# Thirteen runs of 128x128 products sent through four column tiles of TensorE

## The chip, the cores and the metric

The kernel runs on one core of a Trainium2 chip. The metric is the time of one execution on the device, in microseconds (us); lower is better. Three timed runs of the kernel before gave 318.03, 318.08 and 318.10 us; their median, 318.08 us, is the time before.

## The reference

Four batches of 12544 tokens of width 128 pass through two attentions against 32 inducing points, and then through a layer with 1024 hidden units that keeps the larger of two products:

```python
def _attn_ref(x, inducing):                  # x: 4 x 12544 x 128, inducing: 32 x 128
    ...
    def mab(q, kv):
        s = scale * (q @ kv.transpose(0, 2, 1))
        s = s - s.max(-1, keepdims=True)
        a = np.exp(s)
        a /= a.sum(-1, keepdims=True) + 1e-09
        return a @ kv
    h = mab(I, x)                            # 32 points look at all tokens
    return mab(x, h)                         # every token looks at the 32 results

def _moe_ref(x, w1, w2, w_out):              # 50176 x 128; d_ff = 1024
    h1 = x @ w1
    h2 = x @ w2
    g = np.maximum(h1, h2)
    return g @ w_out
```

## The kernel before

**Algebra.** The second attention's output is a mixture of the 32 rows of `h`, so `x @ w1` and `x @ w2` behind it are products with 32 rows too. The kernel writes max(h1, h2) as h1 + relu(h2 - h1). The h1 part is linear and is folded into one small matrix `m1`; the relu part needs `hwd`, which is `h` times (w2 - w1), and then `woutp`, the output weights.

**Tiling.** Tokens are handled in chunks of 128. A `Block` holds four quarters of up to four chunks each. Three kinds of work on TensorE concern us, and each uses the 128x128 array in a mode of its own:

- *Column work*: four matmuls, each of 32 weight columns, side by side, writing to four different groups of 32 PSUM partitions. Such are `stage` (L657: scores of a block's tokens), `pool_scores` (L356: scores of the next batch's 32 points) and `pool_accum` (L414 and L433: the sums of the first attention; its matmuls have 128 rows, 32 weight columns and 128 moving columns).
- *Rounds*: `phase` (L1085), up to four matmuls at a time with 32 rows each, side by side in four row tiles, from `hwd` and the block's exponentials `e`. Each fills one PSUM bank with 128x512 numbers. The relu of each bank is written to SBUF in 16 bits by ScalarE (L1102) or VectorE (L1105), whichever the kernel's own clock model expects to be done earlier. A round may also carry the linear part (`m`, `e`: four 32x128 matmuls).
- *Products*: `final_one` (L932), one matmul of a 128x128 block of `relu` as weights with a 128x128 block of `woutp` moving. There are 3136. Eight for each of a group's chunks accumulate in one PSUM bank (`g.ps`), which `evict_group` scales by the softmax's denominators and stores (L964, L971, L989).

**Order.** The instructions of PE, DVE, ACT, POOL and SP stand in the order in which the program writes them. That order is a string written out by hand, `ORDER`: `s` is one `stage`, `c`, `t`, `a`, `r`, `e`, `h`, `w`, `m` are steps of the first attention of the next batch, `x` a transposing DMA of the next batch, `g` the softmax's denominators by a transposing DMA and POOL, `p4.13` one `phase` of four matmuls with a bit mask that says which of them swap their relu engine, and a bare number is that many products:

```python
elif word.isdigit():
    for _ in range(int(word)):
        ready = final_ready()
        keep_busy(ready)
        ck.wait(ready, "relu")
        final_one()
```

`ck` is the clock model. It decides at build time which bank and which relu engine are taken. It counts a switch of mode (`SWITCH`) and 0.0558 us for a product (`PAIR`). There are eight PSUM banks; a matmul that starts a new bank waits by a semaphore for the engine that read the bank last.

Of the kernel before, what the change touches and what calls it, by code (L numbers as in the profile page):

```python
# [131 lines left out]
def kernel(  # L132
# [9 lines left out]
    nc = tc.nc  # L142
# [3 lines left out]
    NJB = J // 128  # L146
# [25 lines left out]
    def bank(shape, dtype=F32, only=None):  # L172
        i = min(range(8), key=lambda j: ck.bank[j]) if only is None else only
        uid[0] += 1
        return i, psum.tile(shape, dtype, name=f"ps{uid[0]}", tag=f"bank{i}", bufs=1)
# [55 lines left out]
    woutp = consts.tile([128, NJB, C], F16, name="woutp")  # L231
# [6 lines left out]
    with tc.manual_schedule(engines={ET.PE, ET.DVE, ET.Activation, ET.Pool, ET.SP}):  # L238
# [402 lines left out]
        state = {}  # L641
# [107 lines left out]
        def dens(blk):  # L749

            blks = [blk]
            if 0 < blk.index < len(blocks) - 1:
                nxt = blocks[blk.index + 1]
                if nxt.staged is not None and nxt.staged <= ck.pe and nxt.rp is None:
                    blks.append(nxt)
            bi, ps = bank([128, 512])
            ck.wait(ck.bank[bi], "den bank")
            uid[0] += 1
            rp = rpp.tile([128, 8, 4], F32, name=f"rp_{uid[0]}", tag="rp")
            n = 0  # L760
            for blk in blks:
                wd = blk.width
                for t in range(wd):
                    nc.tensor.matmul(
                        out=ps[:, 4 * (n + t) : 4 * (n + t) + 4],
                        lhsT=blk.e2[:, 128 * t : 128 * (t + 1)],
                        rhs=ones_q,
                        start=True,
                        stop=True,
                    )  # L770
                blk.rp = rp[:, n : n + wd, :]
                n += wd
            end = ck.run(0.029 * n)
            nc.vector.reciprocal(out=rp[:, 0:n, :].rearrange("p t q -> p (t q)"), in_=ps[:, 0 : 4 * n])
            ck.bank[bi] = ck.on_dve(end, 0.18 + 0.001 * 4 * n)
# [89 lines left out]
        def final_ready():  # L865
            if state["g"] >= len(groups):
                return INF
            g = groups[state["g"]]
            if g.ps is None and (g.blk.staged is None or len(held) >= HELD):
                return INF  # L870
            t0, u = g.parts[state["mm"] // 4]
            r = g.blk.done.get((g.q, t0, u))
            if r is None:
                return INF
            if g.ps is None:
                r = max(r, min(ck.bank))
            return r
# [25 lines left out]
        def linear_full():  # L903

            g = held[0]
            if st[g.blk.b].get("m1r", INF) > ck.pe or "m1" not in st[g.blk.b]:
                return False
            for s, (q, t) in enumerate(g.chunks):
                nc.tensor.matmul(
                    out=g.ps[:, 128 * s : 128 * (s + 1)],  # L910
                    lhsT=g.blk.e2[:, 128 * t : 128 * (t + 1)],
                    rhs=m1bd[:, q, :],
                    start=False,
                    stop=True,
                    skip_group_check=True,
                )
            evict_group(held.pop(0), ck.run(0.056 * len(g.chunks)))
            return True

        def final_one():  # L920
            g = groups[state["g"]]
            n = len(g.chunks)
            if g.blk.rp is None:
                dens(g.blk)
            if g.ps is None:
                g.bank, g.ps = bank([128, 512])
                ck.wait(ck.bank[g.bank], "group bank")
                ck.bank[g.bank] = INF
            jb, t = g.order[state["mm"]]
            c = g.chunks.index((g.q, t))  # L930
            w4 = g.blk.quarters[g.q].w
            nc.tensor.matmul(  # L932
                out=g.ps[:, 128 * c : 128 * (c + 1)],
                lhsT=g.blk.relu[g.q][:, 128 * (jb * w4 + t) : 128 * (jb * w4 + t + 1)],
                rhs=woutp[:, jb, :],
                start=not g.started,
                stop=(state["mm"] + 1 == n * NJB and g.linear),
                skip_group_check=True,
            )
            g.started = True  # L940
            end = ck.run(ck.PAIR)
            state["mm"] += 1
            state["done"] += 1
            if state["mm"] == n * NJB:
                if g.linear:
                    evict_group(g, end)
                else:
                    held.append(g)
                    if g.full:
                        linear_full()  # L950
                state["g"] += 1
                state["mm"] = 0
# [159 lines left out]
        state["stage"] = 1  # L1112
        ORDER = """
        s p4.13 s H1 W g2 p4.1 p2 8 m0 4 p3 p2.1 10 p3 p2 13 p3.2 6 p4.5 22 p2 p4.8 17 x1.0 p4.8 4 g1 11
        p4.1 13 p4.9 p1 16 p3.4 p2 14 p4.10 6 x1.1 4 x1.2 x1.3 x1.4 x1.5 x1.6 2 p3.6 s s s s 6 g3 6 p4.5
        14 x1.7 1 x1.8 p4.8 19 p4.10 p2.1 12 x1.9 5 p3 14 p4.4 c1.0 15 p1 p4.5 14 p4.3 g4 13 p4.8 25 p4.6
        p3.2 10 x1.10 17 p2 p3.1 15 c1.1 p4.2 12 t1.1 2 p3 6 p4.2 4 g5 11 c1.2 c1.3 p4.1 18 p4.4 t1.3 21
        p3.5 p3 22 c1.4 p1.1 p4.1 19 p2 p4.8 5 g6 21 p4.2 p2 c1.5 19 r1 a1.1 p3.2 p4 t1.5 19 a1.3 p4.9
        p2.2 29 p3.3 p4 26 p4.1 a1.5 5 p3.1 p2.3 1 e1 11 p4.12 1 h1 17 w1 s s s s p3.2 19 m1 15 p4.6 p3.6
        30 p3.1 p3.3 24 p3 p3.3 27 p3.2 p3.1 20 p4.3 p2 15 s p4.1 18 p2.1 p3 15 g7 g8 7 p3.3 p4.2 9 g9 12  # L1120
        x2.0 3 x2.1 x2.2 s p1.1 p4.4 x2.3 12 p4.5 14 p4.6 14 p4 14 p3 21 p3.6 p4.8 14 g10 4 x2.4 4 x2.5
        x2.6 9 p4.13 s c2.0 14 p4.6 p1 5 x2.7 4 x2.8 13 p3.3 p3.4 23 p4.4 11 c2.1 p4 p1 9 t2.1 4 g11 x2.9
        4 x2.10 10 p4.3 p3 15 c2.2 p3.3 21 p3.1 p3.5 27 p3.3 p3.2 c2.3 19 p4.10 4 g12 4 t2.3 5 p4.1 17
        p3.1 p3.4 16 a2.1 c2.4 p3.1 p3.1 23 p4.4 18 p2.1 p4.9 13 g13 17 p4.9 p3.3 24 a2.3 c2.5 p4.1 p2 7
        t2.5 12 r2 18 p3 p4.2 30 p4.10 p2.2 16 a2.5 p4.3 p3.6 8 e2 10 p4.2 2 h2 21 p3.1 p3.6 11 w2 4 m2
        15 p4.11 s s s 13 p3 p2 12 s p4 15 p2 p3.2 22 p3.5 p3.2 3 x3.0 4 x3.1 19 p3.4 p4.12 25 p3.3 13 p3
        p3.3 27 p3.2 p3.5 12 g15 8 g14 3 p4 11 s s p3.1 p2.2 14 x3.2 4 x3.3 4 x3.4 x3.5 5 p3.1 p4.5 19
        x3.6 17 p3.4 p4.1 23 g16 14 p4.4 p3 27 c3.0 s p3.1 15 x3.7 c3.1 p4.2 p1 x3.8 15 p4.4 21 p3.4 p3 8
        g17 14 p3.3 p2 6 t3.1 12 p4.2 p1 20 p3.4 p3.4 22 p4.10 p2.1 30 p4.3 p3 4 g18 8 x3.9 4 x3.10 7
        c3.2 a3.1 c3.3 p4.3 p2 9 t3.3 15 p4.4 17 p2.1 p4.8 27 p2.2 p4.1 13 g19 18 p3.3 p4.4 10 r3 8 c3.4  # L1130
        c3.5 a3.3 p4.5 20 t3.5 1 p4.8 p2.2 21 p4.4 13 p3.5 p2 1 g20 27 p4.4 p3.3 27 a3.5 p4.8 p2.3 2 e3
        16 h3 14 p3.5 p4.2 10 w3 4 m3 15 s p4.1 9 g21 10 p3.1 p2.1 15 p3.5 s s s 13 p3.1 p3.4 22 p4.8 p1
        27 p4.3 p3 9 g22 13 p2.2 p2 22 p3.2 p4.3 25 s s p3.4 13 p3 p3.3 30 p4.9 p3.2 g23 21 p4.2 20 p4.1
        p2.2 30 p3.4 p4.2 24 s p2 p3.2 12 p4.8 g24 22 p4.6 p2.2 20 p2.1 p3.2 16 p3.1 p2 11 p4.9 21 p4.3 9
        p1 p3 g25 p1 20 p3.1 p3.4 30 p4.8 p3.1 26 p4.8 13 p4.6 13 p4.3 9 g26 13 p3.3 p3 27 p3.5 p2 22 p2
        p4.1 22 p2.2 p4.9 22 p3 p2.1 g27 27 p4.1 p3.2 38 p4.3 p3.1 31 p2 p4.9 22 p2.1 p3.1 24 p3 p4.11 40
        p3.4 p3 21 p4.6 21 p2.1 p3.4 31 p4.4 p4.3 63
        """

        EVICT = "000000000000000000000000101000000000000000000000010000000000000000000010000000000000000000000000000000010000"  # L1140
# [17 lines left out]
        for word in ORDER.split():  # L1158
            if word == "s":
                stage(blocks[state["stage"]])  # L1160
                state["stage"] += 1
            elif word.isdigit():
                for _ in range(int(word)):
                    ready = final_ready()
                    keep_busy(ready)
                    ck.wait(ready, "relu")
                    final_one()
            else:
                WORK[word[0]](*[int(n) for n in word[1:].split(".") if n])
        assert state["g"] == len(groups) and not held and state["stage"] == len(blocks)  # L1170
# [31 lines left out]
```

## Time and profile before

| | value |
|---|---|
| median of three timed runs | 318.08 us (318.03 to 318.10) |
| the profiled execution's own time | 317.76 us |
| its span | 316.0 us |
| TensorE matmul (PE) busy | 308.6 us, 5308 records |
| VectorE (DVE) busy | 274.5 us |
| ScalarE (ACT) busy | 280.2 us |
| GpSimd (POOL) busy | 125.8 us |

The span is the time from the first to the last instruction that the profiler recorded in that execution. PE busy is the union of the recorded spans of all matmuls. Matmuls overlap, and their recorded ends are modelled, so the distance between their starts tells more than their lengths. PEld is the loading of weights, which overlaps the matmuls.

### The profile page before, as it was taken

The numbers are of one execution on the slowest core, as the hardware profiler recorded it, in microseconds if no ns is written. First come the engines' busy times: TensorE is split into PE (matmuls) and PEld (weight loads), VectorE is DVE, ScalarE is ACT, GpSimd is POOL, SyncE is SP. The second block draws the span as 40 slices with busy tenths as digits, with TensorE's granted clock in tenths as the row PEclk, the third lists the DMA queues.
The fourth block names the chain that finished last, engine by engine and source line by source line (L and its number), as shares of the span: only waits on it lengthen the run. The fifth ranks groups of instructions, "written<-read, shape, count | busy, mean of one in ns | idle before, by whom it ended". The sixth has DMA issues, their size and how long they took to land.

```text
span 316.0 us, 12577 instructions
## 1 busy us (share of the span) xinstructions
PE 308.6 (98%) x5308; PEld 239.9 (76%) x5308; DVE 274.5 (87%) x488; ACT 280.2 (89%) x580; POOL 125.8 (40%) x187
## 2 busy tenths in 40 slices
PE   6998999999999999999999999999999999999996
PEld 3885777777877777778877787887868777788885
DVE  2468999999878999988999899989899889999885
ACT  3669999999999999998999989899999999998891
POOL 7363060666620066067510064674406564461500
PEclk9999999999999999999999999999999999999999
DMA  8999999989799999898499999897323233324232
GB/s 203 208 252 205 207 219 146 207 229 230 127 218 245 245 183 174 190 233 207 121 225 252 213 227 215 204 174 203 106 85 118 100 106 118 119 88 140 102 120 101
DMA packets 81336, 55.81 MB, mean 177 GB/s; under 512 B 62816, under 2 KB 66176, under 8 KB 81280
## 3 DMA queue, kind: packets, MB, share of 16 engines
q1 hardware_dynamic: 75312, 41.32, 55.8%
q0 software_dynamic: 5968, 13.70, 22.4%
q8 instruction: 41, 0.67, 0.9%
q14 instruction: 15, 0.12, 0.1%
HBM read 27.28 MB, written 25.69 MB: 168 GB/s over the span
## 4 chain that ended last, share of the span: by engine, by line
PE 94%; DMA 2%; ACT 1%; DVE 1%; issue 1%; POOL 0%; POOLq 0%
PE ps L932 60%; PE ps L1085 23%; DMA xn<-in_x_dram 2%; PE ps L657 2%; PE ps L356 2%; PE ps L414 2%; PE ps L276 1%; PE ps L328 1%; PE ps L292 1%; PE ps L521 0%; DVE relu L1105 0%; PE ps L319 0%; ACT e L669 0%; DVE o L964 0%; ACT e_first L696 0%
## 5 line engine op out<-in xcount | busy, mean ns | idle before, releaser
L1102 ACT ACTIVATE relu<-ps 128x512 f16<-128x512 f32 x470 | 241.0, 627 | 17.5 <-PE ps L1085 16.5
L1105 DVE TENSOR_SCALAR relu<-ps 128x512 f16<-128x512 f32 x314 | 199.7, 684 | 20.6 <-PE ps L1085 19.0
L932 PE MATMUL ps<-woutp,relu 128*128 128x128 f16 x3136 | 203.5, 219 | 0.2
L932 PEld LDWEIGHTS <-relu 128*128 128x128 f16 x3136 | 176.6, 98 | 34.4 <-issue 28.7
L1085 PE MATMUL ps<-e,hwd 32*128 32x512 f16 (+2 forms) x840 | 82.8, 361 | 0.1
L720 POOL TENSOR_TENSOR half<-ed 128x256 f32<-128x256 f16 (+2 forms) x23 | 14.1, 613 | 145.8 <-DMA ed<-e 145.8
L724 POOL TENSOR_TENSOR rd<-den,minus 128x16 f32<-128x16 f32 (+2 forms) x23 | 60.7, 2639 | 1.8
L964 DVE TENSOR_TENSOR o<-ps,rd 128x512 f32<-128x512 f32 (+3 forms) x83 | 53.2, 643 | 3.9 <-PE ps L1085 2.8
L1085 PE MATMUL ps<-m,e 32*128 32x128 f16 x372 | 36.8, 216 | 0.0
L1085 PEld LDWEIGHTS <-hwd 32*128 32x128 f16 x880 | 26.7, 91 | 12.8 <-issue 3.8
L1085 PEld LDWEIGHTS <-e 32*128 32x128 f16 x372 | 22.4, 92 | 10.4 <-issue 2.7
L720 POOL TENSOR_TENSOR half<-half 128x32 f32<-128x32 f32 (+3 forms) x69 | 22.3, 323 | 5.4
L195 POOL DMA_DIRECT2D xn<-in_x_dram x32 | 17.6, 563 | 5.7 <-DMA xn<-in_x_dram 4.3
L280 DVE COPY xT<-ps 128x512 f16<-128x512 f16 (+3 forms) x12 | 5.7, 485 | 8.6 <-PE ps L276 8.6
L964 DVE TENSOR_TENSOR o<-ps,rp 128x512 f32<-128x512 f32 (+3 forms) x20 | 12.8, 642 | 0.0
L369 ACT ACTIVATE eu<-ps 128x512 f16<-128x512 f32 x18 | 11.0, 617 | 0.6 <-PE ps L356 0.3
L669 ACT ACTIVATE e<-ps 128x512 f16<-128x512 f32 (+2 forms) x21 | 11.1, 607 | 0.3 <-PE ps L657 0.2
L283 ACT COPY xT<-ps 128x768 f16<-128x768 f16 (+3 forms) x10 | 5.7, 574 | 4.3 <-PE ps L276 4.2
L276 PE MATMUL ps<-identity,xn 128*128 128x128 f16 x98 | 7.6, 220 | 1.4 <-DMA xn<-in_x_dram 0.9
L657 PE MATMUL ps<-xT,hT 128*32 128x512 f16 (+3 forms) x110 | 8.1, 361 | 0.1
L276 PEld LDWEIGHTS <-xn 128*128 128x128 f16 x98 | 5.5, 97 | 2.9 <-DMA xn<-in_x_dram 1.2
L356 PE MATMUL ps<-xT,inducingT 128*32 128x512 f16 x72 | 6.8, 386 | 0.0
(110 smaller groups left out, 117.7 us busy)
## 6 DMA issues: line engine op xcount, KB each, us to landing
out_dram<-o SPq DMA_DIRECT2D x90, 256.0 KB, 3.0
xn<-in_x_dram POOLq DMA_DIRECT2D x24, 448.0 KB, 10.4
out_dram<-o SPq DMA_DIRECT2D x10, 128.0 KB, 2.9
wf<-in_moe_w_dram POOLq DMA_DIRECT2D x4, 256.0 KB, 6.0
xn<-in_x_dram POOLq DMA_DIRECT2D x4, 224.0 KB, 10.2
xT<-xn SPq DMA_TRANSPOSE x33, 4.4
xf<-in_x_dram SPq DMA_DIRECT2D x1, 512.0 KB, 3.7
xf<-in_x_dram SPq DMA_DIRECT2D x1, 384.0 KB, 4.2
```

The source lines that it names most:

```text
L195: nc.gpsimd.dma_start(out=xn_at[b, i][:, 0:n, :], in_=xr[b, :, k0 : k0 + n, :])
L276: nc.tensor.transpose(ps[:, j, :], xn[:, g + j, :], identity16)
L356: nc.tensor.matmul(out=ps[32 * g : 32 * (g + 1), :], lhsT=inducingT, rhs=xT_tiles[b % 2][:, U * u + 4 * g : U * u + 4 * (g + 1), :], start ...
L657: nc.tensor.matmul(out=ps[32 * q : 32 * (q + 1), 128 * t : 128 * (t + n)], lhsT=hq, rhs=xT[:, c : c + n, :], start=True, stop=True, tile_p ...
L669: nc.scalar.activation(out=blk.e2[:, 0 : 128 * wd], in_=ps[:, 0 : 128 * wd], func=AF.Exp, scale=st[0]["rs"] if blk.b == 0 else scale,)
L720: nc.gpsimd.tensor_tensor(out=dst, in0=cur[:, :, 0:n], in1=cur[:, :, n : 2 * n], op=ALU.add)
L724: nc.gpsimd.tensor_tensor(out=rp[:, 0:wd, :].rearrange("p t q -> p (t q)"), in0=den[:, 0 : 4 * wd], in1=minus1[:, 0 : 4 * wd], op=ALU.pow,)
L932: nc.tensor.matmul(out=g.ps[:, 128 * c : 128 * (c + 1)], lhsT=g.blk.relu[g.q][:, 128 * (jb * w4 + t) : 128 * (jb * w4 + t + 1)], rhs=woutp ...
L964: nc.vector.tensor_mul(osb[:, 0:m, :], g.ps[:, 0 : m * C].rearrange("p (s c) -> p s c", s=m), g.blk.rp[:, t0 : t0 + m, q : q + 1].broadcas ...
L1085: nc.tensor.matmul(**seq.pop(0))
L1102: nc.scalar.activation(out=dst, in_=src, func=AF.Relu)
L1105: nc.vector.tensor_scalar(out=dst, in0=src, scalar1=0.0, scalar2=None, op0=ALU.max)
```

## The change

`final_one` gets an argument. With `narrow=True` a product is written as four matmuls: each takes 32 of the 128 columns of the weight block, the same moving block of `woutp`, and writes its own 32 partitions of the same PSUM bank, with the column tile's position given. A number in `ORDER` with an `n` before it is a run of such products.

```diff
-        def final_one():
+        def final_one(narrow=False):
...
-            nc.tensor.matmul(
-                out=g.ps[:, 128 * c : 128 * (c + 1)],
-                lhsT=g.blk.relu[g.q][:, 128 * (jb * w4 + t) : 128 * (jb * w4 + t + 1)],
-                rhs=woutp[:, jb, :],
-                start=not g.started,
-                stop=(state["mm"] + 1 == n * NJB and g.linear),
-                skip_group_check=True,
-            )
+            relu = g.blk.relu[g.q][:, 128 * (jb * w4 + t) : 128 * (jb * w4 + t + 1)]
+            tiles = [(32 * i, 32 * (i + 1)) for i in range(4)] if narrow else [(0, 128)]
+            for lo, hi in tiles:
+                nc.tensor.matmul(
+                    out=g.ps[lo:hi, 128 * c : 128 * (c + 1)],
+                    lhsT=relu[:, lo:hi],
+                    rhs=woutp[:, jb, :],
+                    start=not g.started,
+                    stop=(state["mm"] + 1 == n * NJB and g.linear),
+                    tile_position=(0, lo) if narrow else None,
+                    skip_group_check=True,
+                )
...
-            elif word.isdigit():
-                for _ in range(int(word)):
+            elif word.lstrip("n").isdigit():
+                for _ in range(int(word.lstrip("n"))):
...
-                    final_one()
+                    final_one(word[0] == "n")
```

In `ORDER` nothing moves; fifteen numbers get an `n`. They make thirteen runs on TensorE, since `g3` and `g5` inside two of them issue nothing there. Their lengths, in order, are 12, 15, 15, 15, 5, 15, 14, 11, 15, 12, 11, 15 and 13: 168 products of 3136. Each run stands between column work on one side and a round on the other. Five come after column work and before a round (`s s s s n6 g3 n6 p4.5`, `c1.0 n15 p1`, `a1.5 n5 p3.1`, `c2.0 n14 p4.6`, `s s s n13 p3.1`), eight after a round and before column work (`p3.1 n15 c1.1`, `p4.2 n4 g5 n11 c1.2`, `p2 n15 s`, `p4.4 n11 c2.1`, `p3 n15 c2.2`, `p2 n12 s`, `p4 n11 s s`, `p3.1 n15 c3.1`, shortened to their neighbours on TensorE). The program has 1008 more instructions on TensorE (168 products, three more weight loads and three more matmuls each). DVE, ACT, POOL and SP have the same instructions with the same waits in the same order, since the clock model is told the same durations.

## The prediction

> **What bounds the kernel now.** I read the page first: busy times, then the chain of waits that ended last.
>
> ```profile
> span 316.0 us, 12577 instructions
> PE 308.6 (98%) x5308; PEld 239.9 (76%) x5308; DVE 274.5 (87%) x488; ACT 280.2 (89%) x580; POOL 125.8 (40%) x187
> PEclk9999999999999999999999999999999999999999
> PE 94%; DMA 2%; ACT 1%; DVE 1%; issue 1%; POOL 0%; POOLq 0%
> ```
>
> TensorE is busy for 308.6 of 316.0 us at the full granted clock, and 94% of the chain is TensorE. So far it looks as if every 0.1 us taken from TensorE came off the end. Before believing it, look at the groups, and at who waits for the rounds (L1085):
>
> ```profile
> L1102 ACT ACTIVATE relu<-ps 128x512 f16<-128x512 f32 x470 | 241.0, 627 | 17.5 <-PE ps L1085 16.5
> L1105 DVE TENSOR_SCALAR relu<-ps 128x512 f16<-128x512 f32 x314 | 199.7, 684 | 20.6 <-PE ps L1085 19.0
> ...
>   DVE relu L1105: 19.0, 57
>   ACT relu L1102: 16.5, 46
> ```
>
> There are 470 + 314 = 784 relu evictions. The last two rows say that only 57 + 46 = 103 of them found their engine idle and waiting for the round. The other 681 came to an engine that was still at an earlier bank. So ScalarE and VectorE run close behind TensorE nearly everywhere, and the banks that a round needs come free at their pace. A matmul that waits for a bank while other row tiles stream doesn't show as idle TensorE, since a tile is busy. That is why 98% busy does not mean that TensorE alone sets the pace.
>
> **The change part by part.** It takes away one mode switch per run, thirteen in all: a run after column work is no longer entered by a switch, a run before column work no longer left by one. It adds 504 matmuls and 504 weight loads. Nothing moves on the other engines, and no DMA is moved past anything. What does a switch cost?
>
> ```profile
> 62.99 0.33 PE L932 MATMUL ps<-woutp,relu 128*128 128x128 f16 x3
> 63.25 0.61 PE L356 MATMUL ps<-xT,inducingT 128*32 128x512 f16 x8
> 63.80 0.41 PE L1085 MATMUL ps<-e,hwd 32*128 32x512 f16 x4
> ...
> 50.17 0.40 PE L356 MATMUL ps<-xT,inducingT 128*32 128x512 f16 x4
> 50.51 1.01 PE L932 MATMUL ps<-woutp,relu 128*128 128x128 f16 x15
> 51.45 0.22 PE L1085 MATMUL ps<-m,e 32*128 32x128 f16 x1
> ```
>
> Columns: start, length, engine, line, operands, count, all in us. In the run of 15, the last product is recorded as about 0.22 long, so it starts 1.01 - 0.22 = 0.79 after the first: 14 distances, 0.056 each. The round starts at 51.45, 0.15 after that last start; less the product's own 0.056, the switch took 0.094. The run that ended before 63.25 had its last start at 62.99 + 0.33 - 0.22 = 63.10; the column work came 0.15 later, again a switch of 0.094. In the column work the two sets start 0.61 - 0.39 = 0.22 apart (0.39 being one set's length, between 0.40 and 0.41 less its spread of 0.01), so the first product at 50.51 came 0.34 - 0.22 = 0.12 after the set's streaming. I take 0.095 for a switch: 13 x 0.095 = 1.24 us. More than that is not on offer, since the switch on the other side of each run stays (63.25 to 63.80 less two sets: 0.11 from column work to round, against 0.094 from product to round).
>
> What does a narrow product cost? The same shape exists in the kernel: L414 has 128 rows, 32 weight columns, 128 moving columns, four side by side.
>
> ```profile
> 73.85 1.24 PE L932 MATMUL ps<-woutp,relu 128*128 128x128 f16 x19
> 75.06 0.63 PE L414 MATMUL ps<-xn,eT 128*32 128x128 f16 x32
> 75.05 0.46 PEld L414 LDWEIGHTS <-eT 128*32 128x32 f16 x32
> L414 PEld LDWEIGHTS <-eT x288: 92/97/97, 75.1 to 226.1; 128*32 128x32 f16 x144
> L932 PEld LDWEIGHTS <-relu 128*128 128x128 f16 x3136 | 176.6, 98 | 34.4 <-issue 28.7
> ```
>
> Nineteen whole products: (1.24 - 0.22) / 18 = 0.0567 from start to start. Eight sets of four: (0.63 - 0.22) / 7 = 0.0586. The difference, 0.002 us, contains the spread of about 0.01 within the last set, so the true one lies between 0 and 0.002: 168 products cost 0 to 0.33 us, and I take the lower half. A weight load of 32 columns is recorded at 97 ns, one of 128 columns at 98 ns; 32 of the former start within 0.46 - 0.10 = 0.36 us, hidden beside the matmuls, so the loads add nothing. The Trainium skill speaks against the change here: TensorEngine Tiling, Restrictions, says that column tiles lose the fast weight load, and TensorE: Matmul & The Clock Gate, LDWEIGHTS, gives a plain load one ns per 1.2 columns. By that rule, if a set's loads had to follow each other, four loads of 27 ns would make 107 ns of a product and the sum would be 168 x 0.051 = 8.6 us worse (an estimate from those pages); the sets at 58.6 ns disagree.
>
> Is the 1.24 us passed on to the end? The work that follows each site decides. Take the first, the run of 12 that ends before 43.98:
>
> ```profile
> 43.20 0.28 PE L932 MATMUL ps<-woutp,relu 128*128 128x128 f16 x2
> 43.34 1.66 ACT L669 ACTIVATE e<-ps,rs 128x512 f16<-128x512 f32 x3
> 43.91 0.73 ACT L669 ACTIVATE e<-ps,rs 128x512 f16<-128x512 f32 x1
> 43.98 0.39 PE L1085 MATMUL ps<-e,hwd 32*128 32x512 f16 x3
> 44.12 0.37 PE L1085 MATMUL ps<-e,hwd 32*128 32x512 f16 x1
> 44.42 0.23 PE L932 MATMUL ps<-woutp,relu 128*128 128x128 f16 x1
> ```
>
> Three of the round's tiles start at 43.98, the fourth only at 44.12. Its bank was last read by the exponential that began at 43.34 and took 0.73: done at 44.07, and with 0.05 for the semaphore the matmul starts. That exponential was begun before the run was half through, and nothing in this change makes it earlier. With the switch gone, the three tiles start 0.095 earlier, the fourth still at 44.12, and the products behind the round still at 44.42, 0.30 after it (a set of 0.22 and a switch). All of the saving at this site turns into a longer wait for a bank. The other kind of site:
>
> ```profile
> 100.53 0.68 DVE L1105 TENSOR_SCALAR relu<-ps 128x512 f16<-128x512 f32 x1
> 100.98 0.40 PE L657 MATMUL ps<-xT,hT 128*32 128x512 f16 x4
> 101.31 0.40 PE L1085 MATMUL ps<-e,hwd 32*128 32x512 f16 x4
> ```
>
> Here the last tile starts at about 101.32 into a bank that VectorE gave up at 101.21, plus 0.05: 0.06 is in hand, so of the 0.095 only 0.06 goes on. I followed each of the thirteen sites in this way through the timeline and the program's semaphores, until the saving was eaten or the trace had no more late bank: eight lose all of it in one of the next rounds (43.20 the first, 236.66 the last of them), and five keep 0.04, 0.06, 0.07, 0.08 and 0.095, which makes about 0.33 us (my estimate from those rows; five that keep something, eight that keep nothing). This is the value I take, with up to 0.05 of it given back for the narrow products, whose extra cost is mostly eaten by the same waits. From the profiled 317.76 (1.76 beyond its span) that is 317.43; the median of the timed runs stands 0.32 above the profiled execution, so the forecast is 318.08 - 0.33 = 317.75.
>
> **The rivals.**
>
> *All of it arrives (faster).* If evictions follow the rounds more closely than I think, because what TensorE does earlier also starts ScalarE and VectorE earlier, up to the whole 1.24 arrives: 316.84, or 316.52 in the profiled execution. For it: the 103 places where an engine waits for a round, 35.5 us in all. Against it: the 681 others, and the fourth tile at 44.12. Chance 0.20, at 316.85 to 317.3.
>
> *TensorE's instructions don't come fast enough (slower).* A narrow product is eight instructions in 56 ns, a whole one two. How dense do matmuls get in this trace?
>
> ```profile
> 153.25 0.63 PE L414 MATMUL ps<-xn,eT 128*32 128x128 f16 x32
> 153.71 0.22 PE L433 MATMUL ps<-xn,et 128*32 128x128 f16 x2
> 153.87 0.40 PE L1085 MATMUL ps<-e,hwd 32*128 32x512 f16 x4
> 75.05:78.05 3.00, 3.00 (x97) 1.00 0.82 262
> ```
>
> The longest dense stretch is 32 + 6 = 38 matmuls (L433 has six; two of them are shown) from 153.25 to 153.87: 16 ns each, about nine and a half products' worth. A run of 15 needs 60. Over a longer stretch the densest is 97 in 3.00 us, 31 ns each, paced by other things, so it only bounds the supply from one side. Suppose that the first nine products come from what is queued and the rest at that pace: 4 x 31 = 124 ns in place of 56. Beyond the ninth the thirteen runs have 3+6+6+6+0+6+5+2+6+3+2+6+4 = 55 products, 55 x 0.068 = 3.7 us; less the 1.24 saved, 2.5 us slower: 320.6. It decides from 1.24 / 55 = 0.0225 more per product, that is at 20 ns for each matmul; at the 16 ns of the short stretch the loss (0.5 us) stays below the saving. Chance 0.23, at 318.8 to 320.6. The Trainium skill, TensorE: Matmul & The Clock Gate, section "Wait — 56ns, not 53.3ns?", states that with hardware decode off the sequencer spends about 62 ns on each MATMUL: by that rule 55 x 0.19 = 10.6 us would be added (an estimate from that page). Its share of this rival's chance is 0.02, since 97 matmuls in 3.00 us are twice that fast.
>
> *The narrow products are a few ns dearer.* At 4 to 10 ns each (0.7 to 1.7 us, more than L414 shows), for reading one moving block four times at once, the gain is spent: 317.9 to 318.5. Chance 0.07.
>
> *The change doesn't do what it says.* If TensorE drained between narrow products and other column work too, no switch would go: 318.1 to 318.4. Against it: from L414 to L433 above, 153.25 to 153.71, eight sets take 0.46 with no gap. Chance 0.02.
>
> **How the numbers follow.** The forecast of 317.75, with a range of its own from 317.4 to 318.2, has 0.48. Some 0.2% (0.64 us) is what a measurement of this kernel can tell from no change. Faster by more than that: the first rival and 0.02 of the forecast's tail, 0.22. Slower by more: the second rival and 0.01 of the third, 0.24. Within: 0.54. The range from 316.9 to 319.7 takes in the whole first rival and the milder half of the second, and leaves out some 0.15.
>
> **What would show it.** In the changed profile: a run of 15 narrow products that takes 0.84 to 0.87 us from first to next work (right), or more with the later products further apart than the first nine (the second rival). Column work next to a narrow run without 0.094 between. Rounds behind the sites whose last tile starts when its bank is released, as before, with an earlier first tile: at the first site the fourth tile still some 0.8 us after the exponential began. ScalarE's and VectorE's waits for L1085 a little shorter than 16.5 and 19.0. I am wrong in the main step if the distance from the fourth tile to the run's start stays as it was, so that the end moves by over 0.64 us.

## The result, and the profile after

The changed kernel takes 318.55 us (median of 20 runs, 317.90 to 319.20); the kernel before, run beside it, 317.88 us (20 runs, 317.64 to 318.26). The ratio is 1.0022, with a 95% interval from 1.0016 to 1.0029: 0.67 us slower. The forecast was 0.33 us faster. The ratios here rest on all runs and not on the medians, so the two can differ by some 0.1%.

The page of the kernel after: span, busy times, granted clock, the instruction queue's row (packets, MB, share of 16 engines), the chain, and the groups of the rounds' relu and of the products.

```profile
span 316.6 us, 13585 instructions
...
PE 308.4 (97%) x5812; PEld 239.6 (76%) x5812; DVE 274.0 (87%) x488; ACT 280.0 (88%) x580; POOL 126.0 (40%) x187
...
PEclk9999999999999999999999999999999999999999
...
q8 instruction: 45, 0.74, 1.0%
...
PE 90%; DMA 5%; POOL 1%; ACT 1%; issue 1%; DVE 1%; POOLq 0%
...
L1106 ACT ACTIVATE relu<-ps 128x512 f16<-128x512 f32 x470 | 241.1, 628 | 18.7 <-PE ps L1089 17.6
L1109 DVE TENSOR_SCALAR relu<-ps 128x512 f16<-128x512 f32 x314 | 199.2, 683 | 20.7 <-PE ps L1089 18.9
L935 PE MATMUL ps<-woutp,relu 128*128 128x128 f16 (+1 forms) x3640 | 203.8, 219 | 0.9 <-issue 0.7
```

TensorE is busy for 0.2 us less than before (308.4 against 308.6), and the span is 0.6 us longer. So the time is lost while TensorE stands still. The last row says where the most of it is: the products (L935 here, L932 before) have 0.7 us of idle time ahead of them that ended by "issue", that is, with no semaphore to wait for. The sum of the prediction has no place for such a row.

The timelines of TensorE at that place, the kernel before first and the kernel after below it (start, length, operands, count, in us):

```profile
179.18 1.68 PE L932 MATMUL ps<-woutp,relu 128*128 128x128 f16 x27
```

```profile
178.83 0.56 PE L935 MATMUL ps<-woutp,relu 128*128 128x128 f16 x7
180.11 1.29 PE L935 MATMUL ps<-woutp,relu 128*128 128x128 f16 x20 [0.72 <-issue]
```

The view of waits after has it as one of TensorE's longest (us in total, times, longest us):

```profile
PE ps L935 <- issue: 0.7, 1, 0.7
```

It is a run of 27 whole products, which the change does not touch. After the seventh TensorE stops; the eighth starts at 180.11, 0.93 us after the seventh did. To follow the gain and the loss through the execution, compare each matmul's start with that of the same matmul before (the first one of a narrow product stands for the product); places are given by the time before. The lead of the kernel after is 0.10 us at 27 us, before the first narrow run (a difference of the start-up). It rises by about 0.1 at each narrow run and falls back, wholly or in part, in the rounds behind it: 0.31 at 117 us, 0.44 right behind the narrow run at 178.09, 0.36 just before the stall. At the stall it turns into a lag of 0.52. Behind it the lag falls to 0.34, at 216.18 it grows again by 0.24, at column work of the first attention whose weight loads wait for a transpose (eT), and at the end it is 0.59. So the change gained 0.25 us up to the stall and some 0.18 behind it; it lost 0.88 at the stall and 0.24 at 216.18. In all it is some 0.7 us slower in this pair of executions.

Why does TensorE stop there? The queue that the page calls "instruction" brings the program to the engine. Before, it carried

```profile
q8 instruction: 41, 0.67, 0.9%
```

41 packets of 0.0163 MB each; the page before counts 5308 matmuls and as many weight loads, 10616 instructions. With 1008 more it is 45 packets: about 256 instructions to a packet. Counted on from the stalled product in steps of 256 instructions, the trace falls into blocks; how well that count fits is said with the experiments. By the DMA records the packet of the block that begins at the stall ran from 177.36 to 178.58, although TensorE had entered the block before it at 173.51. The packet lands 0.6 us before the block is reached, and TensorE goes on 1.5 us after the packet landed. So landing alone isn't enough: by this count, of the 564 blocks that begin after 27 us in the fourteen profiles of this document, none begins less than 1.37 us after its packet landed. The views by windows show what else the DMA queues did (length, busy us and counts of PE, PEld, DVE, ACT and POOL, granted clock, DMA share, GB/s):

```profile
172.00:179.00 7.00, 7.00 (x152) 5.15 (x150) 6.04 (x11) 7.00 (x15) 0.00 (x0) 1.00 1.19 184
262.00:276.00 14.00, 14.00 (x223) 10.64 (x221) 12.81 (x21) 13.51 (x28) 7.96 (x12) 1.00 0.34 109
```

From 172 to 179 us, while the last batch of x is loaded, the packets' time adds up to 1.19 times that of the 16 DMA engines, which fits packets that wait for each other. Later, from 262 to 276 us, it is 0.34. More isn't shown of what held this packet back: the last packet of the x load had ended at 176.36, and until 177.36 the engines were full of other packets. In the kernel before the block begins 72 instructions later in the work, at 181.74, and its packet landed at 179.19, 2.5 us ahead of it.

The Trainium skill (Runtime: NRT & Kernel Launch, section "Instruction fetch mechanics") states that instructions are streamed in 16 KiB blocks of 256 by the sequencer's own DMA queue while the block before executes, and that crossing a block is "mostly hidden". The packets agree with the size; this trace shows where it isn't hidden.

### The profile page after: what moved, and what is told of

Its sections match the earlier page's. It is cut to its first block, busy times and chain, and to the rows that moved or that the text cites. A ratio compares the mean times of both kernels' runs of the same rounds, so it can differ in the third digit from the quotient of the medians.

```text
span 316.6 us, 13585 instructions
## 1 busy us (share of the span) xinstructions
PE 308.4 (97%) x5812; PEld 239.6 (76%) x5812; DVE 274.0 (87%) x488; ACT 280.0 (88%) x580; POOL 126.0 (40%) x187
## 4 chain that ended last, share of the span: by engine, by line
PE 90%; DMA 5%; POOL 1%; ACT 1%; issue 1%; DVE 1%; POOLq 0%
PE ps L935 59%; PE ps L1089 23%; DMA xn<-in_x_dram 4%; PE ps L657 2%; PE ps L414 2%; DMA eT<-eu 1%; PE ps L356 1%; POOL xn L195 1%; PE ps L276 1%; DVE relu L1109 0%; PE ps L521 0%; PE ps L328 0%; ACT e L669 0%; DVE o L968 0%; ACT e_first L696 0%
## 5 line engine op out<-in xcount | busy, mean ns | idle before, releaser
L1106 ACT ACTIVATE relu<-ps 128x512 f16<-128x512 f32 x470 | 241.1, 628 | 18.7 <-PE ps L1089 17.6
L1109 DVE TENSOR_SCALAR relu<-ps 128x512 f16<-128x512 f32 x314 | 199.2, 683 | 20.7 <-PE ps L1089 18.9
L935 PE MATMUL ps<-woutp,relu 128*128 128x128 f16 (+1 forms) x3640 | 203.8, 219 | 0.9 <-issue 0.7
L935 PEld LDWEIGHTS <-relu 128*128 128x128 f16 (+1 forms) x3640 | 177.1, 98 | 35.0 <-issue 29.1
```

The costliest lines, as they stand in the source:

```text
L935: nc.tensor.matmul(out=g.ps[lo:hi, 128 * c : 128 * (c + 1)], lhsT=relu[:, lo:hi], rhs=woutp[:, jb, :], start=not g.started, stop=(state["m ...
L1106: nc.scalar.activation(out=dst, in_=src, func=AF.Relu)
L1109: nc.vector.tensor_scalar(out=dst, in0=src, scalar1=0.0, scalar2=None, op0=ALU.max)
```

## The experiments

The theory to test, **supply**: the added instructions use the blocks up sooner, and while a batch of x loads, the next block comes late. Its rival, **narrow products are slow**: the prediction's second one, or a cost of the narrow form itself. The results of `e1` added a third, **late transposes** (a transpose here is a transposing DMA of SP): a packet of instructions that starts during one makes it late, and a late one stalls TensorE.

### Which of the runs, and the same dose in two places

`e1` keeps the `n` on eight runs outside the heaviest loading, `e2` on the other five: 113 and 55 narrow products (the expectations miscount them as 118 and 50). `e3` and `e4` have thirteen whole runs as before, and instead 64 products narrow between rounds, where no switch is saved: 384 more instructions within 11 and 15 us, once during a load, once where none runs.

```diff
 e1: n only in   c1.0 n15 p1   p3.1 n15 c1.1   p4.2 n4 g5 n11 c1.2   c2.0 n14 p4.6   p4.4 n11 c2.1   p3 n15 c2.2   p3.1 n15 c3.1   s n13 p3.1
 e2: n only in   s n6 g3 n6 p4.5   a1.5 n5 p3.1   p2 n15 s   p2 n12 s   p4 n11 s
 e3: before, and  p4 n15 p2   p3.2 n22 p3.5   p3.3 n27 p3.2    (164 to 175 us)
 e4: before, and  g24 n22 p4.6   p3.2 n16 p3.1   p3.1 n26 p4.8  (261 to 277 us)
```

> Eight of the thirteen runs narrow (the second, third, fourth, seventh, eighth, ninth, twelfth and thirteenth: 118 products, 708 more instructions), none of them while a batch of x is loading; the five others whole. Theory S (supply): TensorE's instructions are fetched by DMA in blocks of 256; while a batch loads, a fetch takes 4 to 5 us from request to start against 1 to 2 us otherwise, and narrow runs use a block up sooner, so that TensorE runs dry at a block's end. Here no block should be late: the saved switches that pass the banks, about 0.18 us, so 0.1 us to 0.3 us faster than before and no stall of TensorE without a semaphore. Rival N (each narrow product is dearer by the 6 ns that 1.0 us over 168 products would make): 118 x 0.006 = 0.7 us less 0.2, so 0.5 us slower than before. Rival W (earlier TensorE moves the transposes and stores into each other): a loss in proportion to the switches, 8/13 of 0.67, so 0.4 us slower.

> The complement: only the first, fifth, sixth, tenth and eleventh run narrow (50 products in 5 runs, 300 more instructions), four of them while a batch of x loads or has just been loaded. Theory S: a stall of 0.1 to 0.7 us near 179 to 180 us, in the same batch load as with all thirteen; against 0.06 to 0.15 us saved, so 0.0 to 0.55 us slower than before, in spite of less than a third of the narrow products. Rival N: 50 x 0.006 = 0.3 less 0.15: 0.15 us slower. Rival W: 5/13 of 0.67: 0.25 us slower. With this one the place of the stall tells more than the time.

> The thirteen runs whole as before; instead three runs of 15, 22 and 27 products between two rounds are narrow (64 products, 384 more instructions), at 164 to 175 us, while the last batch of x loads. A switch stays on both sides of each, so no switch is saved; only the number of instructions changes. Theory S: 5 to 6.5 us slower, in two or three stalls of 2 to 4 us between 165 and 183 us, since the blocks come at 256 per about 6.5 us there. Rival N: 64 x 0.006 = 0.4 us slower. Rival W: no switch saved, nothing moves earlier: no change.

> The same dose as the run before (64 narrow products in runs of 22, 16 and 26 between two rounds, 384 more instructions, no switch saved), but at 261 to 276 us, where no batch of x loads. Theory S: blocks are fetched with 5 us to spare there and each run takes up to 3.7 us of it, so no stall: within 0.1 us of before. Rival N: 0.4 us slower, as at the other place. Rival W: no change. It also shows whether 104 narrow matmuls in a row (a run of 26) keep 56 ns for each four, longer than the 60 of the change.

Measured, beside the kernel before at 318.05: `e1` 319.10 (ratio 1.0029, 1.0009 to 1.0049), `e2` 319.54 (1.0044, 1.0021 to 1.0067), `e3` 323.58 (1.0169, 1.0141 to 1.0196), `e4` 318.19 (0.9999, 0.9986 to 1.0012). The timeline of `e3`, its rows by windows for the stop and the time behind it, and the timeline of `e4`:

```profile
166.04 1.36 PE L935 MATMUL ps<-woutp,relu 128*32 128x128 f16 x84
170.67 0.30 PE L935 MATMUL ps<-woutp,relu 128*32 128x128 f16 x4 [3.27 <-issue]
```

```profile
167.40:170.67 3.27, 0.00 (x0) 0.00 (x0) 0.58 (x1) 0.22 (x1) 0.00 (x0) 0.83 1.07 251
170.67:176.80 6.13, 6.13 (x62) 4.45 (x63) 3.22 (x6) 3.22 (x7) 0.00 (x0) 0.53 1.17 217
```

```profile
261.61 1.41 PE L935 MATMUL ps<-woutp,relu 128*32 128x128 f16 x88
...
265.27 1.08 PE L935 MATMUL ps<-woutp,relu 128*32 128x128 f16 x64
...
275.19 1.63 PE L935 MATMUL ps<-woutp,relu 128*32 128x128 f16 x104
```

The same dose costs 5.5 us during the load and nothing outside it, where the tightest block began 1.80 us after its packet landed. In `e4` 104 narrow matmuls take 1.63 us: less the 0.22 of the last one, 1.41 for 25 distances from set to set, 0.056 each, what a whole product takes. That ends the theory of slow narrow products, for runs much longer than the change has. In `e3` TensorE stops for 3.27 us, after 21 of a run's 22 products. Behind that stop the granted clock (the first of the last three numbers) is 0.53 for 6 us; no other stop stands there, so I put the other 2.4 of the profile's 5.9 us down to it.

`e2` stalls one product ahead of where the change stalls. It has 55 narrow products by then, 330 instructions more than the kernel before, where the change has 840; counted in blocks of 256, its block begins two instructions earlier, which is that one product. The stall of `e3` fits the same count: it begins a block, 1024 instructions earlier in its program than the stalled block of the change. The timeline of `e2`:

```profile
179.03 0.51 PE L935 MATMUL ps<-woutp,relu 128*128 128x128 f16 x6
180.29 0.90 PE L935 MATMUL ps<-woutp,relu 128*128 128x128 f16 x13 [0.75 <-issue]
```

`e1` refutes the simple form of the supply theory: it is slower, with no such row. Its losses of 0.4, 0.8 and 0.8 us stand at 82.80, 122.90 and 205.28 of the time before, each at column work of the first attention. The last one, SP's and TensorE's rows in `e1`, and SP's row before:

```profile
202.11 2.78 SPq L395 DMA_TRANSPOSE eT<-eu  x1
...
206.92 0.63 PE L414 MATMUL ps<-xn,eT 128*32 128x128 f16 x32 [0.62 <-DMA eT<-eu]
```

```profile
200.09 1.30 SPq L395 DMA_TRANSPOSE eT<-eu  x1
```

The transposing DMA takes SP 2.78 us to issue in place of 1.30 (it also began 2.0 us later), and a packet of TensorE's instructions began at 202.68, within that time. Over the fourteen profiles, 176 transposes had such a packet starting between 0.3 us before and 1.0 us after their issue: their median is 2.17 us, and 65% took over 1.9. Of the 734 others the median is 1.28, and 10% took over 1.9. This goes together; that the packet is the cause isn't shown. So this is the third theory, and both can be at work. These four runs don't yet show that it is the block's place and not the number of instructions that counts.

### The same program with its blocks shifted, and with lighter loads

`e5` is the change, `e8` the kernel before, each with 36 dummy matmuls of 16 columns (72 instructions) at 25 us, in time that TensorE spends waiting. All block ends shift by 72 instructions, and nothing else changes. `e6` is the change and `e7` the kernel before with each load of the third and fourth batch cut to one of its up to 14 chunks; the rest of that data is left out.

```diff
+            for _ in range(36):                      # e5, e8
+                nc.tensor.matmul(out=ps[:, 0:16], lhsT=warm[:, 0:128], rhs=warm[:, 0:16], ...)
             for jb in range(NJB):
...
-        nc.gpsimd.dma_start(out=xn_at[b, i][:, 0:n, :], in_=xr[b, :, k0 : k0 + n, :])
+        m = n if b < 2 else 1                        # e6, e7
+        nc.gpsimd.dma_start(out=xn_at[b, i][:, 0:m, :], in_=xr[b, :, k0 : k0 + m, :])
```

> The change with all thirteen runs narrow, and the same 72 instructions added near 25 us. Theory S (a block comes too late where a batch loads): the blocks end elsewhere, the one that was late at 180 us has 1 us more; so no stall without a semaphore there. Of the 0.3 us that pass the banks, collisions of fetches with transposes (S2) may take 0 to 0.8 us: 0.3 us faster to 0.5 us slower than before, and different from the 0.67 us of the change. Rival N: as the change, 0.6 to 0.7 us slower. Rival W: as the change.

> All thirteen runs whole, as before; 36 matmuls of 16 columns (72 instructions) are added near 25 us, where TensorE waits about 1 us for ScalarE anyway. No work in the loop changes: only the places in the program where a block of 256 instructions ends move, by 72 instructions or some 2 us. Theory S2 (added after the first four runs: a block's fetch, while it is under way, stretches the issue of a transposing DMA on SP from about 1.3 to 2 us and more, and where that transpose has little to spare, TensorE waits): the fetch that began at 79.87 in the profile of before comes to about 77.8, onto the transpose of eT issued at 77.94, whose matmul at 82.80 had some 0.1 us to spare. So 0.4 to 0.9 us slower than before, with TensorE's wait at L414 for DMA eT. Rival W (only the earlier TensorE matters) and rival N (only narrow products matter): no change, within 0.1 us.

> The change with the loads of batches 2 and 3 cut to one fourteenth of their bytes (the rest of these batches is left as an earlier batch had it, so its result is not the reference's); to be set against the next run, the same cut with the runs whole. Theory S: with the DMA engines free of the batch, a fetch starts within 1 to 2 us everywhere, no block is late, and no stall without a semaphore is seen at 179 us. The pair differs by -0.4 to +0.4 us (saved switches, and collisions with transposes). Rival N: 0.67 us slower than its pair. Rival W: 0.67 us slower than its pair.

> The kernel before with the loads of batches 2 and 3 cut to one fourteenth of their bytes (the rest is left as an earlier batch had it), the other half of the pair. Theories S, N and W all expect about the time before, or up to 1 us less, since some transposes no longer wait for loads.

Measured, beside 318.09 of the kernel before: `e5` 317.94 (ratio 0.9992, 0.9983 to 1.0001), `e8` 318.73 (1.0018, 1.0008 to 1.0029), `e6` 317.86 (1.0002, 0.9987 to 1.0016), `e7` 317.95 (0.9999, 0.9990 to 1.0008). The run of 27 in the timelines of `e5` and `e6`, and `e6`'s row by windows for the time ahead of it:

```profile
179.04 1.68 PE L940 MATMUL ps<-woutp,relu 128*128 128x128 f16 x27
```

```profile
178.86 1.68 PE L936 MATMUL ps<-woutp,relu 128*128 128x128 f16 x27
```

```profile
172.00:179.00 7.00, 7.00 (x153) 5.15 (x151) 6.05 (x11) 7.00 (x15) 0.88 (x2) 1.00 0.65 180
```

Both are unbroken. In `e6` the blocks end exactly where they end in the change, but the DMA share is 0.65 in place of 1.19, and the packet landed at 175.67, 2.9 us earlier than in the change. In `e5` the loads are as heavy as ever (DMA share 1.12 from 172 to 179 us), but the block begins elsewhere, and the packet of that time landed at 175.97. So the stall needs both: a block end at that place, and the load. In `e5` the loop gains 0.25 us over the same products before (a lead of 0.08 at 27 us, of 0.33 at the end), although it loses some 0.17 at 122.90 of the time before, one of `e1`'s three places; SP's transposes (xT) just ahead of it took 4.96 us there in place of 3.97. `e6` gains 0.42 us up to 190 us and then loses 0.5 at 215.15 of the time before, at the work of L380, which waits for a transpose (xT).

`e8` was a surprise. Its median is 0.6 us slower, in the range that the third theory had named, but the wait at L414 that was to cause it isn't in its profile: the loop is at every matmul within 0.01 us of the kernel before. The span is 315.9 and the execution's own time 318.28, so 2.38 lie outside the span, where the other profiles have 1.73 to 1.90. By the DMA records a last packet of instructions ran from 317.58 to 318.53, after the span's end; no other of these profiles has one there. That may explain the one profiled execution. It doesn't explain the median: each run's span is on record, nine of the twelve have the usual 1.7 to 1.8 us outside it, and their spans are 316.2 to 317.6 against a median of 316.35 before. So `e8` loses its 0.6 us inside the span, in executions that weren't profiled, and the cause stays open.

### A whole block, and half a block

If block ends decide, a shift by 256 must bring the stall back, and must leave the kernel before alone. The pad is again 36 dummies at 25 us, and the rest takes the place of some of the warm-up matmuls at the very start.

```diff
-        for _ in range(WARM):
+        for _ in range(WARM - 6):           # 256 instructions: e9 (narrow), e11 (whole); - 2: 128, e10 and e12
             nc.tensor.matmul(out=ps, lhsT=warm[:, 0:128], rhs=warm, start=True, stop=True)
+        for _ in range(98):                 # 30 in e10 and e12
+            nc.tensor.matmul(out=ps[:, 0:16], lhsT=warm[:, 0:128], rhs=warm[:, 0:16], ...)
```

> The change with 256 more instructions on TensorE before its loop (134 dummy matmuls of 16 columns, six warm-up matmuls of 512 columns left out). Instruction-block theory: 256 is one whole block, so the blocks end at the same products as in the change; while the batch of x loads before 180 us runs, the block that begins at the 8th product of the run of 27 comes late again: TensorE stalls 0.5 to 1.0 us there with no semaphore, and the time is 318.3 to 318.8, 0.3 to 0.7 above the whole kernel with the same pad. Rival theory (any additional instruction at the start shifts the loop against the loads and removes the stall, as the pad of 72 did): no stall, 317.7 to 318.0.

> All products whole, with the 256 instructions before the loop. Instruction-block theory: blocks end where they end in the kernel before, so nothing changes: within 0.2 us of it, no stall. If the dummies themselves cost time at the start (later loads, colder warm-up), it is slower by as much as its first product starts later.

> The change with 128 more instructions before the loop, half a block. Instruction-block theory: the block that ended at the 8th product now ends half a block earlier, about 3.3 us before, at a time when its fetch has more to spare; no stall by 180 us, 317.6 to 318.0. If the gain of the pad of 72 was chance (another mechanism at 179 us that any run may or may not meet), the stall is there: 318.3 to 318.8.

> All products whole, with 128 instructions before the loop. The pad of 72 made the whole kernel 0.6 us slower, and its trace shows the loop no later but one more packet of the instruction queue after the last instruction (317.58 to 318.53). If that packet at the end is the cause, the pad of 128 costs nothing unless it shows such a packet too: 317.9 to 318.2. If it is the shifted block ends in the loop (transposes stretched by a fetch), the time is a new draw: slower by 0.3 to 0.8 with a stall of TensorE behind a transpose, or equal without one.

Measured, beside 317.97 of the kernel before: `e9` 319.98 (6 runs, 319.48 to 320.50), `e11` 319.37 (5 runs, 319.23 to 320.08), `e10` 318.15 (ratio 1.0017, 0.9997 to 1.0037), `e12` 318.42 (1.0016, 1.0003 to 1.0029). The dummies at the start weren't free, the second case of `e11`'s expectation: the first product starts 1.72 us later in `e11` and 1.24 in `e9`. So the comparison to make is within the loop. The run of 27 in `e9`, and in `e11`:

```profile
180.16 0.56 PE L945 MATMUL ps<-woutp,relu 128*128 128x128 f16 x7
181.28 1.29 PE L945 MATMUL ps<-woutp,relu 128*128 128x128 f16 x20 [0.55 <-issue]
```

```profile
180.91 1.68 PE L945 MATMUL ps<-woutp,relu 128*128 128x128 f16 x27
```

The stall is back, between the same two products. From the first product on, `e9` gains 0.26 us up to the stall, loses 0.72 there, and ends 0.49 later against the kernel before; `e11` keeps its distance to within 0.02 us from the first product to the last. The stalled product lies 256 instructions later in the program than in the change, one block. By the timed medians `e9` stands 0.61 above `e11`, near the change's own 0.67. With the pad of 72 the narrow kernel stands 0.8 below its whole twin (0.25 in the profiled loops, since the loss of `e8`'s median isn't in its profile), with 256 it stands 0.6 above: one and the same edit.

Half a block (`e10`) also avoids the stall at 180 us, and in its median ends 0.27 below `e12`, within what their intervals allow to be nothing. But its profiled execution stalls elsewhere. SP's and TensorE's rows of `e10`, then SP's of the kernel before:

```profile
55.36 4.69 SPq L208 DMA_TRANSPOSE xT<-xn  x2
...
66.56 3.28 SPq L208 DMA_TRANSPOSE xT<-xn  x1
...
78.79 0.63 PE L414 MATMUL ps<-xn,eT 128*32 128x128 f16 x32 [0.89 <-DMA eT<-eu]
...
84.46 0.63 PE L414 MATMUL ps<-xn,eT 128*32 128x128 f16 x32 [0.28 <-DMA eT<-eu]
```

```profile
54.91 2.68 SPq L208 DMA_TRANSPOSE xT<-xn  x2
...
65.16 2.89 SPq L208 DMA_TRANSPOSE xT<-xn  x1
```

Packets of instructions began at 56.30 and 66.71, both within a transpose's issue. SP's queue ran 1.8 us late at 74 us, and the transposes behind it made TensorE wait 1.3 us longer at two places. The loop ends 0.78 later than before in that execution. This second effect may be a draw that differs between executions of one kernel: `e10`'s runs span 317.74 to 321.12, though its two longest also have a lower granted clock (0.989). One execution of each kernel was profiled, so that isn't shown. The stall at 180 us was in both profiles of a narrow kernel whose blocks ended there under the full load, the change and `e9`.

`e12` settles nothing about `e8`. Its median lies above the 317.9 to 318.2 that its expectation gives for a packet at the end as the cause; yet its loop keeps the kernel before's distances to 0.03 us, and its last packet lies inside the span. Its profiled execution (319.68) starts its products 1.83 us later, with the clock at half for 3.4 us during the start-up. There `e10` and `e12` also have the row of the stall: at 15.8 us L319 waits 0.5 and 0.2 us for "issue", 1.4 us after a block's packet landed.

## Why the prediction was right or wrong

**The switch.** Right. In the kernel before a run of 11 at 177.37 is followed by the scores at 178.09; after, the narrow run follows in 0.62 us in place of 0.72. The two timelines, before and after:

```profile
177.37 0.79 PE L932 MATMUL ps<-woutp,relu 128*128 128x128 f16 x11
178.09 0.61 PE L657 MATMUL ps<-xT,hT 128*32 128x512 f16 x8
```

```profile
50.30 1.01 PE L935 MATMUL ps<-woutp,relu 128*32 128x128 f16 x60
...
177.03 0.80 PE L935 MATMUL ps<-woutp,relu 128*32 128x128 f16 x44
177.65 0.61 PE L657 MATMUL ps<-xT,hT 128*32 128x512 f16 x8
```

**The narrow product.** Right. Fifteen of them take 1.01 us (50.30), what fifteen whole ones took before. The rule of the Trainium skill that was weighed against this (TensorEngine Tiling (Array Packing), Restrictions: column tiles lose the fast weight load; 8.6 us by the estimate) doesn't show here, nor do the 62 ns for a MATMUL that the Trainium skill (TensorE: Matmul & The Clock Gate, section "Wait — 56ns, not 53.3ns?") gives with hardware decode off: 60 matmuls in 1.01 us are 17 ns each, 104 in 1.63 us are 16.

**The absorption.** Right, at the site that was worked out, and nearly so in the sum. TensorE's timeline after, at the first site:

```profile
42.98 0.85 PE L935 MATMUL ps<-woutp,relu 128*32 128x128 f16 x48
43.77 0.62 PE L1089 MATMUL ps<-e,hwd 32*128 32x512 f16 x4
44.32 0.79 PE L935 MATMUL ps<-woutp,relu 128*128 128x128 f16 x11
```

The round's first tile starts at 43.77 in place of 43.98, 0.21 earlier: 0.10 of lead that was there, and the switch. Its last tile starts 0.62 - 0.37 = 0.25 after the first, at 44.02, in place of 44.12: the lead of 0.10, and nothing of the switch. The products behind it follow at 44.32, again 0.10 earlier. Over all sites 0.43 us of the 1.24 passed the banks in the change (0.25 before the stall, 0.18 behind it), and 0.42 in `e6`, where no stall comes between; the forecast's sum was 0.33. Read right behind the narrow run at 178.09, the lead has grown by 0.33 too, but that is chance: two sites are still to come, and the first of them passes its 0.095 on. ScalarE's and VectorE's waits for the rounds, forecast as a little shorter than 16.5 and 19.0, are 17.6 and 18.9.

**The step that failed** is the sentence that nothing moves on the other engines and that the change moves no DMA past anything. A thousand more instructions are four more packets, and every later block of TensorE's program begins at another place. The sum put this at nothing; at the one late block it measured 0.88 us, twice the gain of 0.43. Another 0.24 went at 216.18, behind a late transpose; what made that one late stays open. The page before has the "instruction" row with its 41 packets, and the prediction doesn't use it. This account comes from profiled executions, one of each kernel. The timed medians of the change and of `e9` against `e11` agree with it (0.67 and 0.61), but `e8` shows that a shift of the blocks can cost 0.6 us in the median with no narrow product at all, so not every part of the 0.67 need be this stall.

**The second rival** had the sign and the word, instructions that don't come fast enough, but neither the mechanism nor the place. It priced 68 ns for each product beyond the ninth of a run; measured, that is 0. The greater loss is one wait of one block, in a run of whole products, 1.5 us behind the narrow run.

## What to carry to other kernels

An edit that adds instructions to the engine that sets the end adds transfers: count them in blocks of 256, and look at what the DMA queues do when a block runs out, above all in dense stretches of short instructions during a load. A gain of some tenths of a us can be turned over by where the block ends fall, so before such an edit is called bad, shift it by some dummy instructions in idle time and follow the start of each matmul against the same matmul before. Here a shift of 72 instructions turned a loss of 0.67 us into 317.94 against 318.09 (ratio 0.9992, 0.9983 to 1.0001), which isn't shown to be faster than the kernel before. The same shift made the kernel before 0.6 us slower by its median, so a pad has to be tried and can't be chosen by this account.

## What the runs showed of the hardware

- TensorE's program came in packets of 0.0163 MB, some 256 instructions, one block ahead of use. The packet that TensorE waited for in the change ran for 1.22 us, and the product that needed it started 1.5 us after it had landed. No block after 27 us began sooner than 1.37 us after its landing, and the four stalled ones (the change, `e2`, `e3`, `e9`) began 1.37 to 1.53 us after it.
- A packet started between 0.6 us before and 4.4 us after TensorE entered the block before its own: in the median 0.9 us after it for blocks that begin before 180 us, 0.1 for those from 235 us on. (The expectation of `e1` has 4 to 5 us and 1 to 2.)
- Under the x load one late block cost 0.93 us from product to product in the change, and 216 instructions added within 2.7 us cost a stop of 3.27 us (`e3`). Outside the loads the "mostly hidden" of the Trainium skill (Runtime: NRT & Kernel Launch, section "Instruction fetch mechanics") holds: in `e4` no block came late.
- After that stop the granted clock was 0.53 for 6 us. The Trainium skill (TensorE: Matmul & The Clock Gate, section "Part 1: The HAM clock gate") says that the clock falls to half after an idle window of about 3.4 us. Here less was enough: the row of the stop has 0.83 over 3.27 us, which is 1.1 us at half, so the clock fell some 2.2 us into the stop. None of the stalls under 1.3 us after 27 us was followed by half the clock.
- A packet of TensorE's instructions that starts during the issue of a transposing DMA goes with a longer issue on SP: median 2.17 against 1.28 us.
